# Last batch element of a DeltaNet and MLP-mixer kernel: token product by Strassen's scheme, channel products in 15 of 18 blocks over 384 tokens

## The chip, the core and the metric

The kernel runs on one core of one Trainium2 chip. The metric is the device time of one execution in microseconds. A core has a matrix engine (TensorE, "PE" in the profile; its weight loads are shown apart as "PEld"), a vector engine (VectorE, "DVE"), an activation engine (ScalarE, "ACT"), a general engine (GpSimd, "POOL") and a queue that issues DMA transfers (SyncE, "SP"). Each engine works through its own instructions in program order and waits on semaphores for the others. Matrix products land in PSUM, eight banks of 128 x 512 floats; everything else is kept in SBUF.

## The reference

Four batch elements, 8 heads, 768 tokens, head width 48. First a delta-rule recurrence gives `y`; its heads side by side are `x` (768 tokens x 384 channels). Then one mixer block works on each element:

```python
def _moe_ref(x, w_tok1, w_tok2, w_ch1, w_ch2):
    xt = x.transpose(0, 2, 1)
    h = np.maximum(xt @ w_tok1, 0.0) @ w_tok2        # over tokens: 768 -> 256 -> 768
    u = x + h.transpose(0, 2, 1)
    h2 = np.maximum(u @ w_ch1, 0.0) @ w_ch2          # over channels: 384 -> 1536 -> 384
    return (u + h2).astype(np.float32)
```

So an element has four products: the first and the second token product, and the first and the second channel product. All are in 32-bit floats.

## The kernel before

The work is written as Python generators ("jobs"): `k`, `p`, `c`, `d`, `t`, `i`, `f`, `h`, `j`, `v` load and prepare 128 tokens each, `r0` to `r47` are the steps of the recurrence (64 tokens each, twelve for an element), `w` and `s` load, round and sum weights, and `m0` to `m3` are the mixers of the four elements. A long string of job names (`order`, L1189) says which generator emits its next piece. So the order of the instructions on every engine is written out by hand, and no scheduler changes it.

`mixer(b)` (L1006) works on `xb`, the 768 x 384 block of the element as six chunks of 128 tokens:

- The first token product (L1013): 12 matrix products of 128 x 384 columns, into two PSUM banks, one for each half of the 256 hidden values. ACT takes them through a Relu into `r1` (L1021).
- The second token product (L1026): 12 products of 128 x 384; DVE adds each pair to `xb` (L1030).
- Then three pairs of chunks, 256 tokens each. PE transposes a pair (L1036), ACT copies it to `u_t` (L1040), and `forms` (L933) makes eleven sums of its 128 x 128 pieces on DVE (L954).
- The first channel product for a pair (`wide_fast`, L959, for elements 1 to 3): the weights are cut in 3 x 3 blocks and the pair in 3 x 2, and 15 block products stand for 18. Each is four matmuls of 128 columns into one bank, 60 for a pair (L985). The products run in four chains, each accumulating in its own bank; after each product the bank is read into the hidden block `r2`, by ACT as a copy (L994) or by DVE as a sum or difference (L997), and where a part is complete ACT takes the Relu (L1001). A chain's next product waits for that read.
- The second channel product for a pair: seven block products in place of eight, six matmuls of 192 columns each, 42 for a pair (L1115). The sums of hidden pieces that they need (`halves_of` and the difference of `a12`) are made on DVE (L1067), the sums of weights lie in `wc2` beside the weights (its places 4 to 6; one of the four plain blocks, place 1, is overwritten with a difference). DVE adds each result to `xb` (L1044), and SP stores the finished chunk.

`wc2` holds the second channel weights for the second channel product of every element; they were loaded as 64-bit numbers and rounded at the start by `round_weights` (L264): two ACT passes (L279, L280), a shift on DVE (L282) and an integer sum on GpSimd (L286).

In the last part of the program, `m2` (the third element's mixer) fills PE between the last steps of the recurrence, and `m3` follows. The first token product of `m3` stands right behind step `r47`, then the last 42 matmuls of `m2`, mixed with the second token product of `m3`, and then three pairs of `m3` with no other job beside them.

Of the kernel before, what the change touches and what calls it, by code (L numbers as in the profile page):

```python
# [23 lines left out]
def kernel(  # L24
# [51 lines left out]
    NHT = DCH // 128  # L76
    NM = NHT // 2
    DH = DM // 2
    NU = B * NCH
# [5 lines left out]
    work = ctx.enter_context(tc.tile_pool(name="work", bufs=2))  # L85
    mlp_pool = ctx.enter_context(tc.tile_pool(name="mlp", bufs=2))
# [24 lines left out]
    warm = const.tile([128, 129], FP32, name="warm")  # L111
# [22 lines left out]
    G = U // HB  # L134
# [13 lines left out]
    at = 0  # L148
# [47 lines left out]

    wc2 = const.tile([128, NM, 7, DH], FP32, name="wc2")
    FAST = 1
    FT = NHT // 3
    WB = FT * 128  # L200
    wcx = const.tile([128, WB // 2], FP32, name="wcx")
# [804 lines left out]
    def mixer(b):  # L1006

        xb = xbs[b]
        p_1 = [ps_mlp([128, DM], "p_1") for _ in range(NDH)]
        for c in range(NCH):  # L1010
            assert written.issuperset([NQ * b + 2 * c, NQ * b + 2 * c + 1])
            for dh in range(NDH):
                nc.tensor.matmul(  # L1013
                    p_1[dh], piece_of(w1, c, 0)[:, dh * 128 : (dh + 1) * 128], xb[:, c],
                    start=(c == 0), stop=(c == NCH - 1),
                )
            yield
        r1 = []
        for dh in range(NDH):
            r = mlp_pool.tile([128, DM], FP32, name="r1")  # L1020
            nc.scalar.activation(r, p_1[dh], ACTF.Relu)  # L1021
            r1.append(r)
        for c in range(NCH):
            p_h = ps_mlp([128, DM], "p_h")
            for j in range(NDH):
                nc.tensor.matmul(  # L1026
                    p_h, piece_of(w2, j, c * 128)[:, c * 128 : (c + 1) * 128], r1[j],
                    start=(j == 0), stop=(j == NDH - 1),
                )
            nc.vector.tensor_tensor(out=xb[:, c], in0=xb[:, c], in1=p_h, op=ALU.add)  # L1030
            yield

        def turn(u_t, c):
            p_ut = ps_mlp([128, NCB, 128], "p_ut")
            for cb in range(NCB):
                nc.tensor.transpose(  # L1036
                    p_ut[:, cb], xb[:, c, cb * 128 : (cb + 1) * 128], ident
                )
            i = c % 2 * U
            nc.scalar.copy(u_t[:, :, i : i + U], p_ut)  # L1040

        def add(c, half, p):
            e = slice(DH * half, DH * half + DH)
            nc.vector.tensor_tensor(out=xb[:, c, e], in0=xb[:, c, e], in1=p, op=ALU.add)  # L1044

        def store(c, e=slice(0, DM)):
            nc.sync.dma_start(out=out[b, c * 128 : (c + 1) * 128, e], in_=xb[:, c, e])

        def turn_pair(c):
            u_t = mlp_pool.tile([128, NCB, 2 * U], FP32, name="u_t", bufs=1)  # L1050
            for i in range(2):
                turn(u_t, c + i)
                yield
            if b < FAST:
                return u_t, None
            f = yield from forms(u_t)
            return u_t, f

        u_t, t_c = yield from turn_pair(0)
        for c in range(0, NCH, 2):  # L1060

            r2 = mlp_pool.tile([128, NM, 2, 2 * U], FP32, name="r2", bufs=1)
            a11, a12 = r2[:, :, 0, 0:U], r2[:, :, 1, 0:U]
            a21, a22 = r2[:, :, 0, U : 2 * U], r2[:, :, 1, U : 2 * U]

            def combine(out, x, y, op, ms):
                nc.vector.tensor_tensor(out=out[:, ms], in0=x[:, ms], in1=y[:, ms], op=op)  # L1067

            made = []

            def halves_of(ms):
                if not made:
                    made.extend(
                        loads.tile([128, NM, U], FP32, name=n, tag="d64", bufs=3)
                        for n in ("s1", "s2")
                    )
                s1, s2 = made
                combine(s1, a21, a22, ALU.add, ms)
                combine(s2, s1, a11, ALU.subtract, ms)
                combine(a21, a11, a21, ALU.subtract, ms)  # L1080

            if b >= FAST:
                for ms in wide_fast(t_c, r2):
                    if ms is not None:
                        halves_of(ms)
                    yield
            else:
                for m in range(NM):
                    p_c = ps_mlp([128, 2, 2 * U], "p_c")
                    for k in range(2):  # L1090
                        f = 2 * m + k
# [12 lines left out]
                    if m % (NM // 2) == NM // 2 - 1:  # L1104
                        halves_of(slice(m + 1 - NM // 2, m + 1))
                        yield

            s1, s2 = made
            turns = (*range(2, NM), 0, 1) if b >= FAST else range(NM)

            def product(p, a, j, start):
                for i, m in enumerate(turns):
                    block = (2 * m + j // 2,) if j in (0, 2, 3) else (m, "sum", j)
                    assert (id(wc2), *block) in rounded
                    nc.tensor.matmul(  # L1115
                        p, a[:, m], wc2[:, m, j],
                        start=(start and i == 0), stop=(i == NM - 1),
                        skip_group_check=True,
                    )
# [34 lines left out]
            store(c + 1, slice(0, DH) if final else slice(0, DM))  # L1154
            yield


    jobs = {}
# [12 lines left out]
    for t in range(B * NQ):  # L1171
        jobs[f"r{t}"] = recur(t)
    for b in range(B):
        jobs[f"m{b}"] = mixer(b)
    pieces = [
        piece
        for dst, src in ((w1, moe_w_tok1), (w2, moe_w_tok2), (wc1, moe_w_ch1))
# [97 lines left out]
    m2*4 r47 m2*3 r47 m2*8 r47*2 m3*5 m2 m3 m2*10 m3 m2*3 m3*6 m2 m3*3 m2 m3*158  # L1275
    """
    for word in order.split():
        name, _, n = word.partition("*")
# [34 lines left out]
```

## Time and profile before

| | before |
|---|---|
| time, median of 3 runs | 638.75 us (637.23 to 639.49) |
| the profiled execution's own time | 636.35 us |
| its span, first to last instruction | 634.6 us |
| busy share of the span: PE, DVE, ACT, POOL | 96%, 70%, 41%, 17% |
| span from the end of step r47 to the end of the program | 516.4 to 634.6 us |
| GpSimd busy after 480 us | 0.0 us |

The profile is of one execution. A 32-bit matmul stands in it as two records, so 60 matmuls are "x120" and the mean of a record is half a matmul. The view of the chain of waits follows the work that ended last back to the start; the timeline lists instructions of an engine in order of time, with the start, the length, and in brackets the idle time before it and what ended that.

### The profile page before, as it was taken

What the parts mean: (1) busy time and instruction counts of PE and PEld (TensorE: products, weight loads), DVE (VectorE), ACT (ScalarE), POOL (GpSimd) and SP (SyncE); (2) the same over time, 40 slices, a digit from 0 to 9 for tenths busy, and PEclk for the clock granted to TensorE, in tenths of its full rate; (3) what the DMA queues carried; (4) which work ended last, traced back from release to release, by engine and by line L of the source; (5) the groups of instructions that cost most, each with busy time, mean ns of one, the idle gap of its engine ahead of it and who ended that gap; (6) DMA issues with size and microseconds to landing.
All of it is one profiled execution on the core that took longest, in us unless ns stands there. A gap on an engine that the chain in (4) does not pass through costs nothing.

```text
span 634.6 us, 21586 instructions
## 1 busy us (share of the span) xinstructions
PE 609.1 (96%) x9168; PEld 526.0 (83%) x9168; DVE 443.3 (70%) x1132; ACT 258.9 (41%) x631; POOL 108.7 (17%) x147
## 2 busy tenths in 40 slices
PE   9679898999999999999999999999999999999997
PEld 5448676677898988858899999769999978899997
DVE  3986776977889758897969997588627252473643
ACT  6848886436422332215615332244333230223240
POOL 1447364242400211011111110001000000000000
PEclk9988999999999999999999999999999999999999
DMA  9966777555442444435444222311020000000000
GB/s 173 205 132 136 163 155 186 128 125 141 102 120 52 97 108 77 107 76 119 90 91 93 43 84 41 75 17 27 14 50 7 28 1 13 13 1 25 2 26 26
DMA packets 135776, 50.27 MB, mean 79 GB/s; under 512 B 114656, under 2 KB 130144, under 8 KB 135680
## 3 DMA queue, kind: packets, MB, share of 16 engines
q1 hardware_dynamic: 135680, 48.89, 34.7%
q8 instruction: 72, 1.18, 0.8%
q14 instruction: 24, 0.20, 0.1%
HBM read 39.42 MB, written 9.44 MB: 77 GB/s over the span
## 4 chain that ended last, share of the span: by engine, by line
PE 74%; DVE 10%; ACT 5%; DMA 5%; issue 3%; SPq 2%; POOL 0%; DVEq 0%; ACTq 0%; POOLq 0%
PE p_o L1115 26%; PE p_r L985 18%; PE p_c L1093 6%; PE p L1013 4%; PE p_h L1026 3%; PE p_s L855 2%; PE p_y L837 2%; PE p_k L817 2%; DVE x L680 2%; DVE sub L676 2%; PE p_g L442 2%; PE p_warm L227 1%; DMA kst<-in_k_dram 1%; DMA gm<-w_dram 1%; PE p_z L775 1%
## 5 line engine op out<-in xcount | busy, mean ns | idle before, releaser
L1115 PE MATMUL p_o<-wc,r 128*128 128x192 f32 x720 | 127.0, 329 | 0.6 <-ACT u_t L1040 0.6
L1115 PEld LDWEIGHTS p_o<-wc,r 128*128 128x128 f32 x720 | 116.7, 190 | 3.0 <-ACT u_t L1040 1.1
L997 DVE TENSOR_TENSOR r<-r,p_r 128x512 f32<-128x512 f32 x90 | 59.6, 682 | 35.1 <-PE p_r L985 32.9
L1044 DVE TENSOR_TENSOR xb<-xb,p_o 128x192 f32<-128x192 f32 x84 | 29.2, 350 | 59.7 <-PE p_o L1115 59.5
L680 DVE TENSOR_TENSOR x<-x,sub 128x84 f32<-128x84 f32 (+24 forms) x178 | 60.3, 339 | 6.1
L994 ACT COPY r<-p_r 128x512 f32<-128x512 f32 x54 | 31.5, 585 | 80.6 <-PE p_r L985 77.2
L676 DVE TENSOR_TENSOR sub<-x 128x84 f32<-128x84 f32 (+24 forms) x178 | 57.5, 323 | 9.5 <-DMA x<-n_dram 5.6
L1115 PE MATMUL p_o<-wc,s 128*128 128x192 f32 x288 | 51.2, 330 | 0.3 <-DVE xb L1044 0.3
L1093 PE MATMUL p_c<-u_t,wc 128*128 128x256 f32 x216 | 50.5, 385 | 0.0
L416 POOL TENSOR_TENSOR v_st<-v_st,nrm 128x384 f32<-128x384 f32 x24 | 21.0, 874 | 167.7 <-DMA v_st<-in_v_dram 96.1
L1115 PEld LDWEIGHTS p_o<-wc,s 128*128 128x128 f32 x288 | 46.7, 190 | 1.3 <-DVE xb L1044 0.6
L869 ACT ACTIVATE xb<-p_y 64x192 f32<-64x192 f32 x96 | 31.1, 324 | 39.9 <-PE p_y L856 28.9
L1001 ACT ACTIVATE r<-r 128x512 f32<-128x512 f32 x54 | 33.9, 630 | 28.3 <-DVE r L997 28.0
L1093 PEld LDWEIGHTS p_c<-u_t,wc 128*128 128x128 f32 x216 | 39.8, 190 | 5.4
L499 POOL TENSOR_TENSOR mb<-mask_c,cs 128x512 f32<-128x512 f32 x20 | 21.1, 1053 | 117.7 <-DVE cs L478 94.9
L442 PE MATMUL p_g<-kq 48*64 48x128 f32 (+1 forms) x704 | 37.5, 279 | 3.1 <-ACT kq L511 2.4
L985 PE MATMUL p_r<-u_t,wc 128*128 128x128 f32 x288 | 38.5, 277 | 0.0
L985 PE MATMUL p_r<-t_d,wc 128*128 128x128 f32 x288 | 37.5, 281 | 0.3 <-DVE r L997 0.3
L985 PEld LDWEIGHTS p_r<-u_t,wc 128*128 128x128 f32 x288 | 35.3, 192 | 0.3
L985 PEld LDWEIGHTS p_r<-t_d,wc 128*128 128x128 f32 x288 | 34.0, 191 | 1.3 <-DVE r L997 0.4
L1026 PE MATMUL p_h<-r,w 128*128 128x384 f32 x96 | 33.7, 494 | 0.0
L1013 PE MATMUL p<-xb,w 128*128 128x384 f32 x96 | 33.6, 495 | 0.0
(176 smaller groups left out, 1205.0 us busy)
## 6 DMA issues: line engine op xcount, KB each, us to landing
d<-in_moe_w_ch_dram SPq DMA_DIRECT2D x24, 384.0 KB, 4.0
v_st<-in_v_dram SPq DMA_DIRECT2D x96, 48.0 KB, 2.8
out_dram<-xb SPq DMA_DIRECT2D x23, 192.0 KB, 1.9
kst<-in_k_dram SPq DMA_DIRECT2D x64, 48.0 KB, 3.0
n_dram<-gm SPq DMA_DIRECT2D x72, 32.0 KB, 1.9
pads<-in_k_dram SPq DMA_DIRECT2D x24, 96.0 KB, 3.4
pads<-in_q_dram SPq DMA_DIRECT2D x24, 96.0 KB, 2.7
gm<-w_dram SPq DMA_DIRECT2D x72, 32.0 KB, 2.1
```

The lines of the kernel that those rows point to most:

```text
L442: nc.tensor.matmul(p_g[PAR[i ^ cc], p], kqt[f, p, cc, 0], kqt[f, p, cc])
L676: nc.vector.tensor_tensor(out=tmp, in0=col.to_broadcast(dims), in1=row.to_broadcast(dims), op=ALU.mult,)
L680: nc.vector.tensor_tensor(out=new, in0=new, in1=tmp, op=ALU.add)
L869: nc.scalar.mul(y[:, :, D * i : D * i + D], p_y[PAR[1 - i]], 1.0 if c else -1.0)
L985: nc.tensor.matmul(p[:, i], pieces[i // width][:, at : at + 128], f[f"u{n}"], start=first and i == 0, stop=True, skip_group_check=True,)
L994: nc.scalar.copy(o, p)
L997: nc.vector.tensor_tensor(out=o, in0=o, in1=p, op=ALU.add if sign > 0 else ALU.subtract)
L1001: nc.scalar.activation(o, o, ACTF.Relu)
L1013: nc.tensor.matmul(p_1[dh], piece_of(w1, c, 0)[:, dh * 128 : (dh + 1) * 128], xb[:, c], start=(c == 0), stop=(c == NCH - 1),)
L1026: nc.tensor.matmul(p_h, piece_of(w2, j, c * 128)[:, c * 128 : (c + 1) * 128], r1[j], start=(j == 0), stop=(j == NDH - 1),)
L1093: nc.tensor.matmul(p_c[:, k], piece_of(wc1, cb, f * 128)[:, f * 128 : (f + 1) * 128], u_t[:, cb], start=(cb == 0), stop=(cb == NCB - 1),)
L1115: nc.tensor.matmul(p, a[:, m], wc2[:, m, j], start=(start and i == 0), stop=(i == NM - 1), skip_group_check=True,)
```

## The change

For the last element alone, `mixer` is replaced by `last_mixer`. The other elements are as before.

- **First token product**: `x` in 2 x 2 blocks (chunks 0 to 2 and 3 to 5, columns 0 to 191 and 192 to 383), seven block products of three matmuls of 128 x 192 each, 21 matmuls for 12 of 384 columns. Weight sums are made on GpSimd (job `A`), sums of `x` on GpSimd for all chunks but the last, on DVE for that.
- **Channel products**: two groups of 384 tokens in place of three pairs of 256. The first product is the same 15 of 18 blocks at 192 columns; since four times 192 columns don't fit one bank, each chain has two banks. The second product takes 15 of 18 blocks as well, of 128-token, 512-value and 192-column blocks, in place of seven of eight.
- **Sums for them**: sums of the transposed `u` for the first group on DVE, for the second group on GpSimd; sums of the second channel weights (job `Q`, 12 of 128 x 768) on GpSimd; sums of the hidden blocks (15 of 128 x 512 for a group) on GpSimd, but four of the second group's on DVE.
- **Weights loaded again**: place 1 of `wc2` holds a difference, so jobs `G0` to `G2` load half the columns of half the weights again (six DMAs), round them on ACT and DVE and write them with GpSimd. The write may come only when `m2` has read place 1 for the last time.

```diff
@@ mixer @@
-            final = (b, c) == (B - 1, NCH - 2)
-            if final:
-                store(c + 1, slice(DH, DM))
+            if b == last - 1:
+                o_done.append(True)
...
+    def restore(m):
...
+        for k in range(2):
+            nc.sync.dma_start(out=d64[:, k], in_=rows[:, m + k, 0, DH:DM])
+        yield
...
+        nc.scalar.activation(a, a, ACTF.Prelu, scale=2.0**-112, alpha=2.0**32)
+        nc.scalar.activation(lo, lo, ACTF.Copy, scale=2.0**-29)
+        yield
+        nc.vector.tensor_scalar(
+            out=f, in0=hi, scalar1=3, scalar2=None, op0=ALU.logical_shift_left,
+        )
+        yield
+        assert len(o_done) == 3
+        nc.gpsimd.tensor_tensor(
+            out=wc2[:, m : m + 2, 1].bitcast(U32), in0=f, in1=lo, op=ALU.add
+        )
...
+    def out_sums():
...
+            ("u12", b[1, 0], b[2, 0], add), ("u10", b[0, 0], b[2, 0], add),
+            ("u6", b[0, 1], b[0, 0], sub), ("u3", b[0, 1], b[1, 1], add),
+            ("u2", "u3", b[0, 0], sub), ("u4", b[1, 0], "u2", sub),
+            ("u5", b[0, 0], b[2, 1], add), ("u13", "u12", b[2, 1], sub),
+            ("u8", "u13", b[1, 1], sub), ("u7", none, b[0, 1], sub),
+            ("u7", "u7", b[2, 1], sub), ("u15", b[2, 0], b[2, 1], sub),
...
+            eng = nc.vector if out in SUMS_V else nc.gpsimd
...
+    SUMS_V = ('none',)
+    FORMS_V = (('none',), ('w15', 'w9'))
+
+    ORDER = (
+        (1, 1, ((0, 0, 1, 0),)), (4, 12, ((0, 0, -1, 0),)), (2, 5, ((2, 0, 1, 0),)),
+        (1, 2, ((0, 1, 1, 0),)), (4, 13, ((0, 1, -1, 0),)), (2, 6, ((2, 1, 1, 0),)),
+        (1, 3, ((1, 1, 1, 0),)), (4, 14, ((2, 1, 1, 0),)), (1, 4, ((1, 0, 1, 0),)),
+        (2, 7, ((1, 1, 1, 1),)), (3, 10, ((1, 0, 1, 1), (2, 0, -1, 0))),
+        (2, 8, ((2, 1, -1, 1),)), (4, 15, ((2, 0, 1, 1),)), (3, 11, ((0, 0, 1, 1),)),
+        (2, 9, ((0, 1, 1, 1),)),
+    )
+
+    def last_mixer():
...
+        def wide(q, f):
...
+                if first:
+                    ps = {1: ps_mlp, 4: ps_seq, 2: ps_prep, 3: ps_mlp}[chain]
+                    banks[chain] = [ps([128, 2, DH], f"q_r{chain}") for _ in range(2)]
...
+                    nc.tensor.matmul(
+                        banks[chain][i // 2][:, i % 2],
+                        pieces[i // width][:, at : at + 128], f[f"u{n}"],
+                        start=first and i % 2 == 0, stop=True, skip_group_check=True,
+                    )
+                yield
+                for j, e, sign, fin in reads:
+                    for h, p in enumerate(banks[chain]):
+                        o = hid[q][j][:, 2 * h : 2 * h + 2, DH * e : DH * e + DH]
+                        if (j, e) not in begun:
+                            assert sign == 1
+                            nc.scalar.copy(o, p)
+                        else:
+                            tt(v, o, o, p, add if sign > 0 else sub)
...
+        def a_forms(q):
...
+                tt(v if out in by_v[q] else g, f[out], x, y, op)
...
+        def outs(q, f):
...
+                    nc.tensor.matmul(
+                        p, f[f"w{n}"][:, i], o_w[f"u{n}"][:, i // 2, i % 2],
+                        start=first and i == 0, stop=True, skip_group_check=True,
+                    )
+                yield
+                for j, e, sign, fin in reads:
+                    c = HT * q + j
+                    o = xb[:, c, DH * e : DH * e + DH]
+                    tt(v, o, o, p, add if sign > 0 else sub)
...
@@ order @@
-    m2*16 r45*4 m2*6 j23 m2 v23 m2 r46*4 m2*2 r46*2 m2*2 r46*3 m2*6 r47 r46 r47*4
+    m2*10 A*4 m2*6 r45*4 m2*6 m3*2 j23 m2 v23 m2 m3 r46*4 m2*2 r46*2 m2*2 m3 r46*3
+    m2*6 r47 r46 G0 G1 G2 r47*4 m2*4 m3*2 r47 m2*3 G0*2 r47 m2*4 G1*2 m2*4 G2
...
```

Where the change moves instructions, three places matter. **ACT around step r47.** `L870` (before: `L869`) writes the step's result to `xb`, `L1002` (before: `L1001`) is the Relu of `m2`'s last hidden block, `L848` (before: `L847`) copies the step's `w_t`. Before:

```order
L1001 ACTIVATE r_7307<-r_7307 128x4x128 x2
L847 COPY w_t<-p_w 128x192
L1001 ACTIVATE r_7307<-r_7307 128x4x128 x4
L869 ACTIVATE xb<-p_y 64x4x48 x2
L1021 ACTIVATE r_7543<-p_7486 128x384
```

In the change, at the same place:

```order
L1002 ACTIVATE r_7311<-r_7311 128x4x128 x2
L1232 ACTIVATE pads<-pads 128x384
L1233 ACTIVATE pads<-pads 128x384
L848 COPY w_t<-p_w 128x192
L1002 ACTIVATE r_7311<-r_7311 128x4x128 x2
L1232 ACTIVATE pads<-pads 128x384
L1233 ACTIVATE pads<-pads 128x384
L1002 ACTIVATE r_7311<-r_7311 128x4x128 x2
L1232 ACTIVATE kq_99<-kq_99 128x384
L1233 ACTIVATE kq_99<-kq_99 128x384
L870 ACTIVATE xb<-p_y 64x4x48 x2
```

The six passes that round the reloaded weights (L1232, L1233) now stand between the Relus, one pair of them ahead of `w_t` and all ahead of the write of `xb`. On DVE the shifts of `G0` and `G1` (L1235) stand between the reads of the same hidden block, `G0`'s ahead of the last four reads and `G1`'s ahead of the last two.

**PE behind step r47**, whose last products are `p_y`. Before, the 12 matmuls of the token product (`L1013`, two banks in turn) stand between them and `m2`'s last products; the first two of the 12:

```order
L985 MATMUL p_r<-u_t,lent 128x128 x4
L985 MATMUL p_r<-u_t,wc_126 128x128 x4
L856 MATMUL p_y<-w_t,gm 64x48 x8
L1013 MATMUL p_7486<-xb,w_124 128x384
L1013 MATMUL p_7487<-xb,w_124 128x384
```

In the change seven of the 21 matmuls of the token product (`q_a`, `q_b`) stand ahead of these rows, and the rest among `m2`'s last products (`p_o`):

```order
L857 MATMUL p_y<-w_t,gm 64x48 x8
L1118 MATMUL p_o<-wc_127,r_7311 128x192 x6
L1118 MATMUL p_o_7528<-wc_127,r_7311 128x192 x6
L1317 MATMUL q_b<-xb,w_124 128x192
L1317 MATMUL q_a<-gm,kq_99 128x192
L1118 MATMUL p_o<-wc_127,s_7520 128x192 x6
L1317 MATMUL q_b<-gm,kq_99 128x192 x3
L1118 MATMUL p_o_7528<-wc_127,s_7519 128x192 x6
L1317 MATMUL q_a<-gm,w_124 128x192 x3
L1317 MATMUL q_b<-xb,kq_99 128x192 x3
L1118 MATMUL p_o<-wc_127,r_7311 128x192 x6
L1317 MATMUL q_a<-gm,w_124 128x192 x3
```

`m2`'s last products have moved forward, from behind the whole token product to directly behind the step.

**GpSimd at the end.** Before, its last rows are those of `v_st` for step r47; nothing follows. In the change, from that row on (`L1240` the write of reloaded weights, `L1274` job `Q`, the last `L1299` the sums of the second group's `u`; 26 sums of hidden blocks follow):

```order
L417 TENSOR_TENSOR v_st<-v_st,nrm_103 128x384
L1299 TENSOR_TENSOR gm<-xb 128x576
L1299 TENSOR_TENSOR gm<-xb,gm 128x384
L1299 TENSOR_TENSOR gm<-xb 128x384
L1299 TENSOR_TENSOR gm<-xb,gm 128x384
L1240 TENSOR_TENSOR wc_127<-pads 128x2x192
L1240 TENSOR_TENSOR wc_127<-gm,pads 128x2x192
L1274 TENSOR_TENSOR gm<-wc_127 128x768 x4
L1274 TENSOR_TENSOR gm<-gm,wc_127 128x768
L1274 TENSOR_TENSOR gm<-wc_127,gm 128x768
L1240 TENSOR_TENSOR wc_127<-gm,kq_99 128x2x192
L1274 TENSOR_TENSOR gm<-wc_127 128x768
```

The third `L1240` reads what DVE's third shift (L1235) makes, and that shift stands on DVE behind the eleven sums of the first group's `u`, so GpSimd stops there after six sums of job `Q` until those are made.

More of the change, by code (lines that the diff above doesn't have):

```diff
@@ L198 @@
     FAST = 1
+    last = B - 1
     FT = NHT // 3
@@ L1153, in mixer, with cut_of @@
             add(c + 1, 0, p_o)
-            store(c + 1, slice(0, DH) if final else slice(0, DM))
+            store(c + 1)
             yield
+    a_sums = {}
+    R3 = NCH // 2
+    HT = 3
+    gm_flat = gmb.rearrange("s b n -> s (b n)")
+    kq_flat = [kq.rearrange("f i p e n -> f (i p e n)") for kq in kq_of]
+    pads_flat = pads.rearrange("s i e n -> s (i e n)")
+    def cut_of(flat, at, shape):
+        n = 1
+        for x in shape:
+            n *= x
+        flat = flat[:, at : at + n]
+        if len(shape) == 1:
+            return flat
+        if len(shape) == 2:
+            return flat.rearrange("p (a n) -> p a n", a=shape[0])
+        return flat.rearrange("p (a b n) -> p a b n", a=shape[0], b=shape[1])
@@ new lines, in winograd_a, with token_sums @@
+    def winograd_a(out, a11, a12, a21, a22):
+        s1, s2, d = out
+        for o, x, y, op in (
+            (s1, a21, a22, ALU.add), (s2, s1, a11, ALU.subtract),
+            (d, a12, s2, ALU.subtract), (a21, a11, a21, ALU.subtract),
+        ):
+            nc.gpsimd.tensor_tensor(out=o, in0=x, in1=y, op=op)
+            yield
+        return
+    def token_sums():
+        u = last * NCH + 1
+        assert token_done and 2 * u + 1 in keyed and u in asked
+        assert turned.issuperset(((True, NU - 1), (False, NU - 1)))
+        x, a = a_sums[1]["sums"], a_sums[1]["raw"]
+        for i, _ in enumerate(winograd_a(x, *a)):
+            if i == 3:
+                a_sums["made"] = True
+            yield
@@ new lines @@
+    o_w = {}
+    def out_sums():
+        assert walked.issuperset(range(B * NQ))
+        b = {
+            (k, e): wc2[:, 2 * k : 2 * k + 2, e:4:2] for k in range(3) for e in range(2)
+        }
+        names = ("u5", "u12", "u3", "u2", "u6", "u13", "u4", "u8", "u10")
+        n = 4 * DH
+        f = {z: cut_of(gm_flat, i * n, (2, 2, DH)) for i, z in enumerate(names)}
+        f.update(
+            u7=b[0, 1], u15=b[2, 0], u1=b[0, 0], u9=b[1, 1], u11=b[1, 0], u14=b[2, 1]
+        )
+        add, sub = ALU.add, ALU.subtract
+        none = warm[:, 0:1][:, None, None, :].to_broadcast([128, 2, 2, DH])
+        for out, x, y, op in (
+            ("u12", b[1, 0], b[2, 0], add), ("u10", b[0, 0], b[2, 0], add),
[4 more added lines that the diff above has]
+            ("u7", "u7", b[2, 1], sub), ("u15", b[2, 0], b[2, 1], sub),
+        ):
+            assert len(whole) >= {"u12": 0, "u10": 0, "u6": 1}.get(out, 2)
+            assert len(whole) == 3 or y is not b[2, 1]
+            x, y = (f[z] if isinstance(z, str) else z for z in (x, y))
+            eng = nc.vector if out in SUMS_V else nc.gpsimd
+            eng.tensor_tensor(out=f[out], in0=x, in1=y, op=op)
+            o_w.update({z: f[z] for z in ("u1", "u9", "u11", "u14")})
+            if x is not none:
+                o_w[out] = f[out]
+            yield
@@ L1173 @@
     for b in range(B):
-        jobs[f"m{b}"] = mixer(b)
+        jobs[f"m{b}"] = mixer(b) if b < last else last_mixer()
+    jobs["A"] = token_sums()
+    for i in range(3):
+        jobs[f"G{i}"] = restore(2 * i)
+    jobs["Q"] = out_sums()
     pieces = [
```

271 lines of the change are left out of this document (270 added, 1 removed).

## Prediction

> **What bounds the kernel now.** I read the page first, then the chain of waits over the part that the change touches, then the timeline at its gaps.
>
> ```profile
> span 634.6 us, 21586 instructions
> PE 609.1 (96%) x9168; PEld 526.0 (83%) x9168; DVE 443.3 (70%) x1132; ACT 258.9 (41%) x631; POOL 108.7 (17%) x147
> ```
>
> PE is busy nearly always, so time is won by fewer or cheaper matmuls, and every wait put in front of PE costs its full length. The chain of waits (start, length, what) from the end of step r47 on:
>
> ```profile
> 516.45 7.94 PE p L1013 x24
> 524.39 8.78 PE p_o L1115 x54
> 537.38 6.45 PE p_h L1026 x20
> 543.83 0.33 PE p_ut L1036 x3
> 546.44 13.67 PE p_r L985 x120
> 563.01 12.07 PE p_o L1115 x72
> 575.08 13.67 PE p_r L985 x120
> 591.65 12.07 PE p_o L1115 x72
> 603.73 13.68 PE p_r L985 x120
> 617.43 0.70 DVE r L997
> 621.57 10.03 PE p_o L1115 x60
> 631.62 0.35 DVE xb L1044
> ```
>
> From this a record of 192 columns costs 8.78 / 54 = 0.1626 us, of 128 columns 13.67 / 120 = 0.1139, of 384 columns 6.45 / 20 = 0.3225; a transpose costs 0.11. The chain runs over DVE from 617.43 to 621.57, but PE isn't idle there, as the timeline says:
>
> ```profile
> 563.01 2.22 PE L1115 MATMUL p_o<-wc,r 128*128 128x192 f32 x12 [0.29 <-ACT u_t L1040]
> 617.23 4.07 PE L1115 MATMUL p_o<-wc,r 128*128 128x192 f32 x24
> 621.57 4.17 PE L1115 MATMUL p_o<-wc,s 128*128 128x192 f32 x24 [0.27 <-DVE xb L1044]
> ```
>
> PE did 24 records meanwhile and lost 0.27 us. It loses 0.29 us for `u_t` in each of the first two pairs. That is all the visible waiting after r47, so little is to be won from gaps.
>
> **What goes.**
>
> - First token product: 7.94 us now; 21 matmuls are 42 records, 42 x 0.1626 = 6.83. Gain 1.11.
> - First channel product: 360 records of 128 columns take 13.67 + 13.67 + 13.68 = 41.02 us; 120 matmuls of 192 columns are 240 records, 39.02. Gain 2.00. The columns are as many (360 x 128 = 240 x 192); the gain is that short records cost more for a column.
> - Second channel product: 126 matmuls become 120, 12 records less. Gain 1.95.
> - Waits seen: 2 x 0.29 + 0.27 = 0.85. Behind each group's products PE now finds the other group's.
> - Slower stretches: 72 records took 12.07 against 72 x 0.1626 = 11.71, twice, and the last 60 took 10.03 against 9.76; together 0.99. They stand at changes of bank. New code has many such changes, so I take half, 0.5; bounds 0 and 1.0.
>
> Together 6.4 us. The second token product stays, and so do the 18 transposes.
>
> The Trainium skill ("TensorE: Matmul & The Clock Gate", Back-to-back issue gap) gives N / 2.4 + 2.5 ns as the gap of a single warm matmul; if a record counts as two, my estimate is 0.112 us at 128 columns and 0.165 at 192, so that the second item would gain 0.6 us instead of 2.0. The trace's 0.1139 and 0.1626 differ from that in both directions, and the trace decides.
>
> **What comes: ACT and DVE at step r47.** Seven matmuls (14 records, 2.28 us) stand ahead of the step's last products, so everything there comes 2.28 us later; that is paid inside the 6.83 above. The timeline there, before:
>
> ```profile
> 511.41 0.63 ACT L1001 ACTIVATE r<-r 128x512 f32<-128x512 f32 x1 [1.10 <-DVE r L997]
> 513.11 0.63 ACT L1001 ACTIVATE r<-r 128x512 f32<-128x512 f32 x1 [1.07 <-DVE r L997]
> 513.65 0.30 ACT L847 COPY w_t<-p_w 128x192 f32<-128x192 f32 x1
> 517.27 0.66 ACT L869 ACTIVATE xb<-p_y 64x192 f32<-64x192 f32 x2
> 512.39 3.30 DVE L997 TENSOR_TENSOR r<-r,p_r 128x512 f32<-128x512 f32 x5 [1.01 <-PE p_r L985]
> 514.80 1.06 PE L985 MATMUL p_r<-u_t,wc 128*128 128x128 f32 x8
> 516.38 2.85 PE L1013 MATMUL p<-xb,w 128*128 128x384 f32 x8
> ```
>
> What a rounding costs, from the same instructions at the start of the program (min/median/max ns):
>
> ```profile
> L279 ACT ACTIVATE d<-d x34: 427/558/572, 4.4 to 166.2; 128x384 f32<-128x384 f32 x28, 128x256 f32<-128x256 f32 x6
> L280 ACT ACTIVATE d<-d x34: 417/548/579, 4.8 to 166.7; 128x384 uint32<-128x384 uint32 x28, 128x256 uint32<-128x256 uint32 x6
> L282 DVE TENSOR_SCALAR w_f<-d x34: 282/352/704, 4.9 to 170.0; 128x384 uint32<-128x384 uint32 x28, 128x256 uint32<-128x256 uint32 x6
> ```
>
> So a pair of ACT passes takes 1.11 us and a DVE shift 0.35. Working the queues through:
>
> 1. The second Relu ends at 513.74 + 2.28 = 516.02. `G0`'s passes follow, to 517.13; DVE's shift, to 517.48; only then DVE's read of the block product whose bank the last product needs (0.66), to 518.14. That product stood at 514.80 + 2.28 = 517.08. **PE waits 1.06 us**, and the step's products end at 516.38 + 2.28 + 1.06 = 519.72.
> 2. DVE's next read ends at 518.80, two Relus at 519.45, `G1`'s passes at 520.56, the shift at 520.91, the last two reads at 521.57 and 522.23, the Relus for them at 522.20 and 522.88. PE has begun `m2`'s last products at 519.72, does four matmuls (1.30 us) and needs the fifth Relu. **It waits 1.2 us**, where before the token product's 7.94 us covered this.
> 3. `G2`'s passes end at 523.99, the write of `xb` at 524.65. The first matmul on the last chunk needs it at about 524.8: no wait. The next needs a sum on DVE, which stands behind six sums of hidden blocks; these rows time them, from 618.04 to 621.16:
>
> ```profile
> 618.04 0.68 DVE L1067 TENSOR_TENSOR s<-r 128x512 f32<-128x512 f32 x1
> 620.83 0.42 DVE L1067 TENSOR_TENSOR r<-r 128x256 f32<-128x256 f32 x1
> 621.16 0.81 DVE L1044 TENSOR_TENSOR xb<-xb,p_o 128x192 f32<-128x192 f32 x2
> ```
>
> 3.12 us from 522.23 is 525.35; an add and the sum (about 0.3 each) bring it to 525.98, and PE has been free since 525.15. **It waits 0.8 us.**
>
> Together 3.1 us. The bounds are 0 (if the passes slip into ACT's idle 1.10 and 1.07 us) and 6.3 (if a rounding's passes and shift, 1.46 us, and one more Relu, 0.63, held PE at each of the three places). I take the worked 3.1, as its rows come from this very stretch. The DMAs for the reload are issued after `m2`'s second pair is stored, about 499 us; that 1.2 MB is due at 516, on queues that are nearly empty.
>
> After that a product has its sums in time. In the first channel product DVE reads two banks of 128 x 384, each about 0.55 by the `p_h` adds below, 1.1 us for a product that takes PE 8 x 0.1626 = 1.30.
>
> ```profile
> L1030 DVE TENSOR_TENSOR xb<-xb,p_h 128x384 f32<-128x384 f32 x6 | 3.3, 554 | 5.9 <-PE p_h L1026 5.9
> ```
>
> **GpSimd.** These groups price it (mean ns before the bar's end):
>
> ```profile
> L286 POOL TENSOR_TENSOR wc<-w_f,d 128x384 uint32<-128x384 uint32 x24 | 25.3, 1061 | 40.9 <-DVE w_f L282 18.1 <-ACT d L280 6.7 <-issue 5.7
> L499 POOL TENSOR_TENSOR mb<-mask_c,cs 128x512 f32<-128x512 f32 x20 | 21.1, 1053 | 117.7 <-DVE cs L478 94.9 <-DVE gm L445 21.9 <-DMA d<-in_moe_w_tok_dram 0.8
> L416 POOL TENSOR_TENSOR v_st<-v_st,nrm 128x384 f32<-128x384 f32 x24 | 21.0, 874 | 167.7 <-DMA v_st<-in_v_dram 96.1 <-DMA gm<-w_dram 20.6 <-DVE t_d L954 18.7
> L286 POOL TENSOR_TENSOR w<-w_f,d 128x256 uint32<-128x256 uint32 x6 | 4.4, 735 | 19.4 <-ACT d L280 9.6 <-ACT wc L491 9.2 <-ACT gm L731 0.6
> ```
>
> 128 columns more cost 1053 - 874 = 179 ns in float and 1061 - 735 = 326 in the strided integers. That puts 768 columns at 1.4 to 2.0 us and 512 at 1.05 to 1.4. No row shows two dense float inputs; both ends stay. Some 5 us after the first group's first product starts, GpSimd goes on with a write (1.1), job `Q`'s other six sums (8.4 to 12.0) and the first of eleven sums of 192 columns (under 0.9, the 256-column row plus its slope); that one is due 21 us after the same start and comes at 15 to 19, the other ten are wanted 1.3 us apart. The first group's 15 hidden sums take 16 to 21, beside 19.5 us of PE in the second group's product; the first is wanted at its end, and the last 18 us later. So GpSimd costs nothing in the forecast.
>
> **The sum.** Gain 6.4, loss 3.1, net 3.3 us: the profiled execution's 636.35 us (1.75 around its span) would be 633.0. The median of the runs is 2.4 us above that execution, so the median becomes 638.75 - 3.3 = **635.4 us**; by the bounds of the forecast's own terms 632 to 638.7.
>
> **Rivals.**
>
> *The sums on VectorE meet GpSimd* (the slower side). The rows show what a meeting costs:
>
> ```profile
> 121.04 0.40 DVE L680 TENSOR_TENSOR x<-x,sub 128x234 f32<-128x234 f32 x1
> 121.84 2.16 POOL L286 TENSOR_TENSOR wc<-w_f,d 128x384 uint32<-128x384 uint32 x2 [5.69 <-issue]
> 122.05 1.08 DVE L680 TENSOR_TENSOR x<-x,sub 128x228 f32<-128x228 f32 x1
> 123.06 0.68 DVE L445 TENSOR_TENSOR gm<-p_g,mb 128x512 f32<-128x512 f32 x1
> ```
>
> With both inputs in SBUF a DVE sum of 0.40 took 1.08 beside GpSimd, ending with GpSimd's instruction; with one input in PSUM (`p_g`) it took its usual 0.68. The Trainium skill ("SBUF — State Buffer", SBUF: two separate sides) has it as an exclusive lock on a shared port pair, held for a whole instruction, by a GpSimd operation or a VectorE one with two SBUF inputs; the trace agrees. The eleven sums of the first group's `u` have two SBUF inputs. GpSimd may begin the reload's write when `m2` has read place 1 for the last time; from there to DVE's first such sum PE has 30 records of 192, 24 of 384 and nine transposes, 4.9 + 7.7 + 1.0, and an add: 14.2 us. GpSimd has two writes (2.1) and six sums (8.4 to 12.0): 10.5 to 14.1, just clear. They meet from 2.0 us a sum; the GpSimd time left then goes into DVE's queue, of which PE covers about 1 us. From 2.7 us (18.3 in all, 4.1 late) the gain is gone, and at 3.2 (21.3, 7.1 late) 6.1 us are lost: 638.75 - 3.3 + 6.1 = 641.5. Against it: 2.7 is well over the rows' upper end.
>
> *The queues at r47 cost 6.3, not 3.1*: 638.6, no change to speak of. For it: every Relu, read and pass there is in one chain through two queues. Against it: the passes' rows are steady (548 to 572).
>
> *The queues hide them* and all slow stretches go: 638.75 - 6.9 = 631.9. For it: ACT's idle 1.10 and 1.07 us; against it: the passes stand behind Relus in program order.
>
> *The change doesn't get its sums off the path*: the second group's hidden sums come late. They start with the first group's last; 23 sums are wanted within 37 us, so it decides at 1.6 us each, against 1.05 to 1.4. At 1.7 the price is about 2 us, and DVE's four sums there wait too: 638.5.
>
> **Chances.** Forecast 0.62, meeting 0.07, dearer queues 0.14, hidden queues 0.12, late sums 0.05. The range takes the forecast's bounds and reaches to the dearer queues and nearly to the hidden ones: 632.0 to 638.8. A measurement of this kernel tells about 0.3% (1.9 us) from no change: faster takes 0.58 of the forecast's chance and the hidden queues', 0.70; the same takes 0.04 of the forecast's, 0.12 of the dearer queues' and half of the late sums', 0.18; slower the rest, 0.12.
>
> **What would show it.** Right: a span near 631; records of 192 columns at 0.163 in all of `q_r` and `q_o`; three short idle times of PE between r47's end and the second token product, 3 us in all; none over 0.3 us behind it; DVE's eleven sums at about 0.35 each. Wrong: DVE's eleven sums at over 1 us beside GpSimd, PE waiting for POOL at the second group's first products, GpSimd sums of 512 columns over 1.6 us, or the first channel product's records above 0.17.

## The result and the profile after

In the first timing the changed kernel takes 630.93 us (median of four runs, 629.99 to 633.96) against 638.87: a ratio of 0.9888, 95% interval 0.9848 to 0.9928. In a second timing on one chip, beside the experiments, it takes 632.98 (eight runs, 627.8 to 635.15) against 637.6 (25 runs): 0.9926, interval 0.9898 to 0.9954. So the change makes the kernel faster, by 4.6 to 7.9 us by the two medians, where 3.3 was forecast. The profiled execution took 631.77 us:

```profile
span 630.0 us, 21470 instructions
PE 605.4 (96%) x9054; PEld 525.7 (83%) x9054; DVE 437.9 (70%) x1120; ACT 261.9 (42%) x642; POOL 179.8 (29%) x207
```

GpSimd has 71 us more work than before; PE is as full as it was. To compare two kernels I use marks in the chain of waits. Before (first line), and after (the others):

```profile
495.33 3.12 PE p_o L1115 x18
```

```profile
495.81 3.12 PE p_o L1118 x18
...
547.85 1.30 PE q_r L1450 x8
...
552.74 35.10 PE q_r L1450 x216
587.84 39.01 PE q_o L1505 x240
626.88 0.35 DVE xb L1299
```

The first mark is the start of `m2`'s last 18 records ahead of the steps r46 and r47; how far it moves from run to run is shown with the first experiments. The **changed stretch** runs from it to the start of the last add on DVE: before 631.62 - 495.33 = 136.29 us, after 626.88 - 495.81 = 131.07. That is 5.22 us less, in two parts. From the mark to the first wide product it is 52.04 after and 546.44 - 495.33 = 51.11 before: **0.93 us longer**, of which three transposes that stood behind this point before make 0.33. From there to the end it is 79.03 against 85.18: **6.15 us shorter**, and in it 216 and 240 records run at 0.1625 us each with no wait.

What PE waits for around step r47, in the timeline (brackets: idle time and what ended it):

```profile
518.00 1.16 PE L986 MATMUL p_r<-u_t,wc 128*128 128x128 f32 x8 [0.27 <-DVE r L998]
519.68 4.54 PE L1118 MATMUL p_o<-wc,r 128*128 128x192 f32 x24
524.05 0.49 PE L1317 MATMUL q_b<-xb,w 128*128 128x192 f32 x2
524.88 0.59 PE L1317 MATMUL q_a<-gm,kq 128*128 128x192 f32 x2 [0.34 <-DVE gm L1299]
```

The three places of the forecast are there: in front of the last block product 0.27; inside the 24 records that start at 519.68, which reach to 524.05, 4.37 us for 24 x 0.1626 = 3.90, 0.47 lost; and 0.34 for `t5`. Visible are 1.1 us, where 3.1 were forecast.

GpSimd's new work, by group (busy us, mean ns before the bar's end):

```profile
L1274 POOL TENSOR_TENSOR gm<-wc 128x768 f32<-128x768 f32 x5 | 8.9, 1804 | 0.1
L1299 POOL TENSOR_TENSOR kq<-kq 128x512 f32<-128x512 f32 x6 | 7.6, 1274 | 0.2
L1299 POOL TENSOR_TENSOR wc<-wc 128x192 f32<-128x192 f32 x11 | 6.2, 599 | 0.2
```

768 columns take 1.80 us (forecast 1.4 to 2.0), 512 take 1.27 (1.05 to 1.4), 192 take 0.60 (under 0.9). No wait of PE in the changed stretch ends with GpSimd.

### The profile page after: what moved, and what is told of

The parts are those of the page before. It is cut to its first block, busy times and chain, and to the rows that moved or that the text cites. A ratio compares the mean times of both kernels' runs of the same rounds, so it can differ in the third digit from the quotient of the medians.

```text
span 630.0 us, 21470 instructions
## 1 busy us (share of the span) xinstructions
PE 605.4 (96%) x9054; PEld 525.7 (83%) x9054; DVE 437.9 (70%) x1120; ACT 261.9 (42%) x642; POOL 179.8 (29%) x207
## 4 chain that ended last, share of the span: by engine, by line
PE 81%; DVE 7%; DMA 4%; ACT 4%; SPq 2%; issue 2%; DVEq 0%; ACTq 0%
PE p_o L1118 20%; PE p_r L986 11%; PE p_c L1096 7%; PE q_o L1505 6%; PE q_r L1450 6%; PE p L1014 4%; PE p_h L1027 3%; PE p_g L443 3%; PE p_k L818 3%; PE p_s L856 3%; PE p_y L838 3%; PE p_warm L228 2%; DMA kst<-in_k_dram 2%; PE p_w L842 1%; PE p_z L776 1%
## 5 line engine op out<-in xcount | busy, mean ns | idle before, releaser
L1118 PE MATMUL p_o<-wc,r 128*128 128x192 f32 x540 | 96.4, 330 | 0.1
L1118 PEld LDWEIGHTS p_o<-wc,r 128*128 128x128 f32 x540 | 87.5, 190 | 2.2 <-ACT r L1002 0.4
L998 DVE TENSOR_TENSOR r<-r,p_r 128x512 f32<-128x512 f32 x60 | 39.5, 682 | 16.3 <-PE p_r L986 16.0
L870 ACT ACTIVATE xb<-p_y 64x192 f32<-64x192 f32 x96 | 31.1, 324 | 39.2 <-PE p_y L857 28.2
L287 POOL TENSOR_TENSOR wc<-w_f,d 128x384 uint32<-128x384 uint32 x24 | 25.3, 1059 | 42.3 <-DVE w_f L283 14.6
L848 ACT COPY w_t<-p_w 128x192 f32<-128x192 f32 x48 | 15.2, 316 | 46.2 <-PE p_w L842 45.8
L443 PEld LDWEIGHTS p_g<-kq 48*64 48x64 f32 (+1 forms) x704 | 27.1, 135 | 8.4 <-ACT kq L512 3.8
L818 PEld LDWEIGHTS p_k<-s_t,kq 48*64 48x64 f32 x656 | 24.0, 136 | 10.6 <-DVE s_t L865 5.1
L838 PEld LDWEIGHTS p_y<-s_t,kq 48*64 48x64 f32 x656 | 24.3, 136 | 10.0 <-issue 7.0
L818 PE MATMUL p_k<-s_t,kq 48*64 48x48 f32 x656 | 29.5, 225 | 2.7 <-DVE s_t L865 2.6
L446 DVE TENSOR_TENSOR gm<-p_g,mb 128x512 f32<-128x512 f32 x44 | 29.3, 684 | 3.7 <-PE p_g L443 3.1
```

The source lines that it names most:

```text
L443: nc.tensor.matmul(p_g[PAR[i ^ cc], p], kqt[f, p, cc, 0], kqt[f, p, cc])
L818: nc.tensor.matmul(p_k[r, p], kqt[f, p, cc, 0], s0[f, p])
L838: nc.tensor.matmul(p_y[o, p], kqt[f, p, cc, 1], s0[f, p], start=(p == 0), stop=False,)
L870: nc.scalar.mul(y[:, :, D * i : D * i + D], p_y[PAR[1 - i]], 1.0 if c else -1.0)
L998: nc.vector.tensor_tensor(out=o, in0=o, in1=p, op=ALU.add if sign > 0 else ALU.subtract)
L1118: nc.tensor.matmul(p, a[:, m], wc2[:, m, j], start=(start and i == 0), stop=(i == NM - 1), skip_group_check=True,)
```

## The experiments

All kernels but `meet` compute the same thing. The intervals are those of the ratio to the kernel before on the same chip.

**Each kernel once more.** The changed kernel:

> The changed kernel as it stands, in five rounds. Theory A (what the two profiles show in the changed stretch is all there is): from step r45's copy of `w_t`, 486 us, to the end the two profiles differ by 5.1 us, and nothing ahead of that differs by kernel, so the ratio is about 0.992 (-5.1 us), and the stretch takes 143.2 us again. Rival B (the first medians' -7.9 us is the change's own worth, the rest of it somewhere ahead of 486 us): the ratio is about 0.988 again, and the marks ahead of 486 us stand earlier than before's.

The kernel before against itself:

> The kernel before against itself: its ratio should hold 1 within 0.002, and its profile gives a second copy of the early marks. Theory A expects the stretch from step r45's copy of `w_t` to the end at 148.2 us again and the mark itself to differ from 486.35 us by some us of chance; rival B expects that mark at or behind 486 us and after the mark of the changed kernel of the same chip by 2 to 3 us.

The changed kernel has the ratio 0.9926 (0.9898 to 0.9954), the kernel before 1.0004 (0.9982 to 1.0027). In the second profiles the changed stretch is 627.73 - 496.67 = 131.06 us after and 630.83 - 494.53 = 136.30 before, within 0.01 us of the first ones; from step r45's copy of `w_t` to the end it is 143.1 us (487.69 to 630.8) and 148.2 (485.56 to 633.8), as expected. Theory A holds. The mark itself stands at 495.33 and 494.53 in the two profiles of before and at 495.81 and 496.67 in those of the changed kernel, no earlier with the change, so rival B falls. The mark moves with what happens at the start of the program. Two kernels further down, whose code up to there differs in the place of six DMAs and their passes near 480 us alone, have marks 5.07 us apart (493.57 and 498.64), and 4.4 us of that are there at a copy of `w_t` that starts at 144.78 in the one and at 149.16 in the other. The windows view from 0 to 130 us shows that their granted clocks differ (the column ahead of the last two); `token_old`:

```profile
0.00:130.00 130.00, 111.81 (x2322) 82.02 (x2323) 100.25 (x271) 91.77 (x245) 55.54 (x76) 0.96 0.75 161
```

`token_old_early`:

```profile
0.00:130.00 130.00, 112.58 (x2301) 83.76 (x2302) 96.18 (x259) 91.25 (x243) 55.68 (x76) 0.91 0.71 155
```

A twentieth of clock over 130 us is at most 6.5 us. The clock is not all of it: in the two profiles of before the same view has 0.96 and 0.93, and the mark of the second, with the lower clock, is the earlier one. What else moves the mark stays open. That is the noise in which a kernel's time stands; the changed stretch repeats to 0.01 us.

**The reload's passes away from step r47.**

```diff
-    m2*10 A*4 m2*6 r45*4 m2*6 m3*2 j23 ...
-    m2*6 r47 r46 G0 G1 G2 r47*4 m2*4 m3*2 r47 m2*3 G0*2 r47 m2*4 G1*2 m2*4 G2
+    m2*10 A*4 G0 G1 G2 m2*6 r45 G0*2 G1*2 G2 r45*3 m2*6 m3*2 j23 ...
+    m2*6 r47 r46 r47*4 m2*4 m3*2 r47 m2*3 r47 m2*4 m2*4
```

> Changed kernel with the reload's DMAs issued ahead of step r45 and its six ACT passes and the first two DVE shifts moved there, where ACT had 8.7 us of idle time. Theory: PE's waits at r47 (0.27 us in front of the last block product, 0.45 us inside the products behind it, 0.34 us for the sum t5) come from those passes and shifts in the queues; the first two go and the third shrinks, 0.7 to 1.4 us faster than the changed kernel. Rival: Relus and DVE's reads alone make the waits, or the moved loads and passes cost as much at r45: within 0.3 us of the changed kernel.

0.9887 (0.986 to 0.9914); median 629.85 us beside the changed kernel's 632.98 on the same chip. ACT in the new place, and PE behind r47:

```profile
485.98 0.33 ACT L848 COPY w_t<-p_w 128x192 f32<-128x192 f32 x1
486.19 0.58 ACT L1232 ACTIVATE pads<-pads 128x384 f32<-128x384 f32 x1
...
488.43 0.56 ACT L1233 ACTIVATE kq<-kq 128x384 uint32<-128x384 uint32 x1
495.05 0.66 ACT L870 ACTIVATE xb<-p_y 64x192 f32<-64x192 f32 x2 [6.05 <-PE p_y L857]
```

```profile
518.29 4.17 PE L1118 MATMUL p_o<-wc,r 128*128 128x192 f32 x24
522.29 0.49 PE L1317 MATMUL q_b<-xb,w 128*128 128x192 f32 x2
522.62 0.49 PE L1317 MATMUL q_a<-gm,kq 128*128 128x192 f32 x2
```

Six passes end 6 us ahead of the next work of ACT, and the three waits of PE are gone, the third too, which was expected only to shrink (24 records from 518.29 to 522.29 are 0.1 over 3.90). By the chain, the first wide product starts 50.53 us behind the mark, and the stretch is 129.55:

```profile
494.96 3.12 PE p_o L1118 x18
...
545.49 1.30 PE q_r L1450 x8
...
624.51 0.35 DVE xb L1299
```

So the passes cost the changed kernel **1.52 us** (131.07 - 129.55), a little over the 0.7 to 1.4 expected. By PE's timelines, each counted from its mark, the three places cost 0.54, 0.37 and 0.61 us: the first wait is shown as 0.27 us of idle time and costs twice that, the last as 0.34. In their new place the passes and their DMAs stand ahead of the mark, where the stretch doesn't count them. But from an ACT copy ahead of those DMAs (469.80, and 470.65 in the changed kernel) to the mark in PE's timeline (494.89 and 495.74) it is 25.09 us in both, so they cost nothing there. The medians differ by 3.1, and the intervals of the two ratios overlap; the stretch, which repeats, says 1.5. By it this version beats both kernels.

**The old token product**, with the reload late and early:

```diff
-            nc.gpsimd.tensor_tensor(out=o, in0=x, in1=y, op=op)   # job A
...
+        p_1 = [ps_mlp([128, DM], "p_1") for _ in range(NDH)]
+        for c in range(NCH):
+            for dh in range(NDH):
+                nc.tensor.matmul(p_1[dh], w1[:, c, dh * 128 : (dh + 1) * 128], xb[:, c], ...)
```

> Changed kernel with the first token product made as before (24 matmuls of 384 columns behind the reload's passes), the channel products and the reload as changed. Theory: it loses the token product's 1.1 us and gets back only the wait for t5 (0.34 us), so it is 0.5 to 1.0 us slower than the changed kernel. Rival: the new token product's waits eat its gain, as the first wide product's start suggests (0.9 us later than before's): it is as fast, or up to 0.9 us faster.

> The old token product together with the early reload, the fourth corner of a square. From the start of the last 18 output products of the third pair (495.33 us in the profile of before) to the first wide product it is 51.1 us before, 52.0 changed, 50.5 with the early reload, 53.3 with the old token product. Theory (the two edits do not touch each other; old product 7.94, no waits, one more set of three transposes of 0.11 ahead of that mark than before): 51.4 us, 0.9 slower than the new product with the early reload. Rival (the old product hides the queues or meets other waits): 50.5 or less, or 52 and more.

Ratios 0.9958 (0.9937 to 0.9978) and 0.9918 (0.9874 to 0.9963). The chain of `token_old`:

```profile
493.57 3.12 PE p_o L1118 x18
...
546.85 1.30 PE q_r L1414 x8
```

and of `token_old_early`:

```profile
498.64 3.12 PE p_o L1118 x18
...
550.36 1.30 PE q_r L1414 x8
```

From the mark to the first wide product:

| | passes at r47 | passes at r45 |
|---|---|---|
| old token product | 53.28 us | 51.72 us |
| new token product | 52.04 us (the change) | 50.53 us |

The new product is worth 1.24 and 1.19 us, against 1.11 by its records; the passes at r47 cost 1.56 and 1.51, whichever product stands there. The two edits do not touch each other. For the early corner 51.4 was expected and 51.7 came. For the late one I expected a loss of 0.5 to 1.0 us, which was too little: I let the old product win back the wait for `t5`, and it has a wait of its own in place of it, 0.39 us of idle time in front of an output product, for an add of DVE to `xb`.

**GpSimd beside DVE's eleven sums.** The first attempt moved the third reload's write and six weight sums ahead of them:

```diff
-    ... m2*2 G0 G1 Q*6 m3 m2*2 m3*4 m2*2
-    m3*10 G2*2 Q*6 m3*120
+    ... m2*2 G0 G1 Q*6 G2*2 Q*6 m3 m2*2 m3*4 m2*2
+    m3*10 m3*120
```

> Changed kernel with the third reload's shift and write and the last six weight sums of GpSimd put ahead of the eleven DVE sums of the first group in program order, so that GpSimd works on 768 columns while DVE makes them. Theory (a DVE sum with both inputs in SBUF waits for GpSimd's instruction, as at 122.05 us): these sums take over 1 us each beside GpSimd, PE waits for several of them, and the stretch from the first wide product to the end (82.15 us in the changed kernel) grows by 3 to 10 us. Rival (two dense float sums do not meet): sums at 0.35 us and 82.2 us again.

This kernel answers another question: the sums moved stand ahead of `m2`'s last product in program order and overwrite weight blocks that it reads, so that this product is made with other weights, and PE waits for them:

```profile
557.86 1.65 PE L1118 MATMUL p_o<-wc,r 128*128 128x192 f32 x4 [20.58 <-POOL wc L1274]
```

1.0333 (1.0303 to 1.0363). When DVE came to its eleven sums GpSimd was idle; nothing follows on the meeting. The second attempt lengthens GpSimd's work where it stands:

```diff
             eng.tensor_tensor(out=f[out], in0=x, in1=y, op=op)
+            if out in ("u3", "u2", "u4"):
+                eng.tensor_tensor(out=f[out], in0=x, in1=y, op=op)
```

> Changed kernel with three of GpSimd's first six weight sums (`u3`, `u2`, `u4`) issued twice: 5.4 us more from 547.2 us on, so that GpSimd works on 768 columns until 552.7 while DVE makes its eleven sums from 548.4 (in the changed kernel it is idle there). By the forecast's rival of a meeting the GpSimd time left at 548.4 goes into DVE's queue, less 1 us of cover: the stretch from the first wide product to PE's end grows by 3.3 us. By the run with the doubled hidden sums, where a DVE sum beside GpSimd took 1.49 instead of 0.69 us and GpSimd's 1.7 instead of 1.27, the two take turns: three or four sums are made by 553, one is wanted every 1.6 us, and 0.5 to 2 us are lost. If they do not meet: nothing, and sums of 0.35 us.

0.9969 (0.9928 to 1.0009). The timelines of DVE, GpSimd and PE at that place:

```profile
548.87 4.76 DVE L1301 TENSOR_TENSOR a_x<-gm 128x192 f32<-128x192 f32 x3
553.66 0.36 DVE L1301 TENSOR_TENSOR a_x<-a_x,gm 128x192 f32<-128x192 f32 x1
```

```profile
547.81 1.81 POOL L1276 TENSOR_TENSOR gm<-gm,wc 128x768 f32<-128x768 f32 x1
549.71 1.81 POOL L1274 TENSOR_TENSOR gm<-wc,gm 128x768 f32<-128x768 f32 x1
551.60 1.81 POOL L1276 TENSOR_TENSOR gm<-wc,gm 128x768 f32<-128x768 f32 x1
```

```profile
554.07 1.57 PE L1452 MATMUL q_r<-a_x,lent 128*128 128x192 f32 x8 [0.39 <-DVE a_x L1301]
556.81 2.87 PE L1452 MATMUL q_r<-a_x,wc 128*128 128x192 f32 x16 [1.17 <-DVE kq L1301]
```

Three sums of 0.35 us take 4.76 beside GpSimd, one for each of its instructions, and keep their 0.36 when it has ended. By the chain's mark (496.31) and last add (629.91) the stretch is 133.60 us, 2.53 longer: between the two forecasts of a meeting (0.5 to 2, and 3.3). In the changed kernel the last of GpSimd's six sums and DVE's first stand so:

```profile
545.40 1.81 POOL L1274 TENSOR_TENSOR gm<-wc,gm 128x768 f32<-128x768 f32 x1
```

```profile
548.36 0.89 DVE L1299 TENSOR_TENSOR a_x<-gm 128x192 f32<-128x192 f32 x3
```

GpSimd ends at 547.21 (545.40 + 1.81), so they miss each other by 1.2 us.

**Hidden sums: dearer on GpSimd, and all on DVE.**

```diff
                 tt(v if out in by_v[q] else g, f[out], x, y, op)
+                if out in ("w12", "w11", "w3", "w2", "w5"):
+                    tt(g, f[out], x, y, op)
```

> Changed kernel with the first five hidden sums of each group issued twice on GpSimd, 10 instructions of 1.27 us more. Theory (GpSimd works without pause from 570.0 us and the second group's `w1`, 23 sums later, is wanted at 607.35): 33 x 1.27 = 41.9, so `w1` comes at 611.9 and the end is 4.6 us later, all of it as one wait of PE in front of the second group's first output product. Rival (the sums have more slack, or PE waits for other sums first): under 1 us, or waits already in the first group's product.

1.0043 (0.9995 to 1.0091). The timelines of PE, DVE and GpSimd where the second group's output product starts, and the clock there by the windows view:

```profile
612.20 2.93 PE L1507 MATMUL q_o<-wc,r 128*128 128x192 f32 x8 [6.50 <-POOL r L1299]
```

```profile
609.53 1.49 DVE L1299 TENSOR_TENSOR pads<-pads 128x512 f32<-128x512 f32 x1
```

```profile
610.43 1.71 POOL L1299 TENSOR_TENSOR r<-r,pads 128x512 f32<-128x512 f32 x1
```

```profile
612.20:616.60 4.40, 4.40 (x14) 4.40 (x15) 2.52 (x4) 0.00 (x0) 4.32 (x3) 0.50 0.12 45
```

One wait at the place named, with nothing ahead of it; it is 6.50 us long, not 4.6. By the timeline GpSimd's instructions start 1.30 us apart (31 from 568.38 to 608.70), where I took 1.27, and the last two meet DVE's hidden sums: 1.71 us in place of 1.27 on GpSimd, 1.49 in place of 0.68 on DVE. The stretch grew by more than the wait: 634.45 - 494.16 = 140.29, 9.22 us more. Behind the wait PE has half its clock for some 4.4 us (0.50 in the last row), which is where most of the other 2.7 goes.

```diff
-    FORMS_V = (('none',), ('w15', 'w9'))
+    FORMS_V = (h, h)   # h: all the names
```

> Changed kernel with all fifteen hidden sums of both groups on DVE instead of GpSimd. By listed durations DVE has 15 x 0.685 + 20 x 0.552 = 21.3 us to do while PE has 19.5 us of products, so the first group's output product would wait about 1.8 us. By the spacing at which back-to-back DVE instructions start (0.60 for 512 columns, 0.47 for 384) it has 18.4 us, and nothing is lost: within 0.3 us of the changed kernel. The first is the way in which the waits at r47 were forecast, the second the way in which this study explains that they came out smaller.

0.9936 (0.9892 to 0.9979). By mark (497.76) and last add (628.87) the stretch is 131.11 us, 0.04 more than in the changed kernel. DVE's timeline late in the second group's first channel product, beside which it now makes the first group's hidden sums:

```profile
586.34 0.68 DVE L1299 TENSOR_TENSOR kq<-kq 128x512 f32<-128x512 f32 x1
586.94 1.01 DVE L1299 TENSOR_TENSOR pads<-pads,q_r 128x384 f32<-128x384 f32 x2
587.87 0.68 DVE L1299 TENSOR_TENSOR kq<-kq,kq 128x512 f32<-128x512 f32 x1
```

A sum listed at 0.68 is followed by the next instruction after 0.60, two reads listed at 0.55 each by the next after 0.93. Having the sums on GpSimd gains no time here. But the run doesn't decide between the two ways of counting, as was meant. PE starts the first group's output product at 589.63, when DVE has made twelve of the fifteen sums (the last starts at 592.46), and it needn't wait: its first block product reads `w1`, the eighth of them. Eight sums and twenty reads fit into 19.5 us by listed durations too (8 x 0.685 + 20 x 0.552 = 16.5).

## Why the prediction was right and wrong

- **What goes**: right, and only its last term too small. The gains were 1.11 + 2.00 + 1.95 + 0.85 + 0.5 = 6.4 us. With the passes out of the way the change is worth 136.29 - 129.55 = 6.74; so 0.34 more goes than forecast.
- **Slower stretches**: mis-sized. "New code has many such changes, so I take half": 0.5. But 216 and 240 records in a row take 0.1625 each, across all their changes of bank. From the first wide product on, 6.15 us went, 0.33 of it transposes that now stand ahead: 5.82, against 2.00 + 1.95 + 0.85 + 0.99 = 5.79. So the whole 0.99 went. "They stand at changes of bank" was the wrong reason: in before's timeline the last 36 of the 72 records from 563.01 take 5.85 us, 0.1625 each, and most of the excess is what the wait for `u_t` costs over its idle time. Ahead of it six transposes and the wait take 1.11 us (561.90 to 563.01) where 0.66 + 0.29 are listed, and the 12 records behind it 2.06 in place of 1.95. The waits at r47 cost more than their idle time in the same way.
- **What comes at r47**: the step that failed. The mechanism was right: passes and shifts in the queues make PE wait at the three places named, and without them PE doesn't wait. The size was 3.1 us (1.06, 1.2 and 0.8) and is 1.52 (0.54, 0.37 and 0.61). Two things made it too large. The larger is a wait that isn't there: twice the chain puts DVE's shift behind both of ACT's passes ("`G0`'s passes follow, to 517.13; DVE's shift, to 517.48"). By the code of the change the shift reads the high words, which the first pass writes, and the second pass works on the low ones. ACT's and DVE's timelines at r47 in the changed kernel:

```profile
515.87 0.63 ACT L1002 ACTIVATE r<-r 128x512 f32<-128x512 f32 x1 [2.38 <-DVE r L998]
516.41 0.54 ACT L1232 ACTIVATE pads<-pads 128x384 f32<-128x384 f32 x1
516.85 0.55 ACT L1233 ACTIVATE pads<-pads 128x384 uint32<-128x384 uint32 x1
517.30 0.30 ACT L848 COPY w_t<-p_w 128x192 f32<-128x192 f32 x1
```

```profile
516.99 0.36 DVE L1235 TENSOR_SCALAR pads<-pads 128x384 uint32<-128x384 uint32 x1 [0.55 <-ACT pads L1232]
519.68 0.36 DVE L1235 TENSOR_SCALAR gm<-pads 128x384 uint32<-128x384 uint32 x1 [1.14 <-ACT pads L1232]
```

  The first shift starts at 516.99, right behind the first pass (516.41 + 0.54; the bracket names its line, L1232) and before the second ends (516.85 + 0.55). My estimate, the forecast's own chain with its listed durations and the shift behind the first pass alone: waits of 0.5, 0.6 and 0.85, 2.0 us in all. So 1.1 us of the error is this wait. The other 0.5 fits the second thing, though no run tests it by itself: I added listed durations, and a listed duration is not the time until the next start. A pair of passes is listed at 1.09 and delays the next instruction by 0.89; a Relu of 0.63 by 0.54; a DVE sum of 0.68 by 0.60. The Trainium skill says it in two places: "Perfetto Trace Analysis" (Optimizing Scalar/DVE Operations) has half of the fixed latency that a profile shows for an instruction overlapping with the next one, and "Vector Engine (DVE) Microarchitecture Reference" (5.2, Measured stream behaviour on trn2) gives 1.0417 ns a column and about 75 ns for back-to-back DVE instructions; my estimate by that page is 0.61 us for 512 columns and 0.475 for 384, and the rows' 0.60 and 0.47 agree.
- **The sum**: 6.74 - 1.52 = 5.22 us in place of 6.4 - 3.1 = 3.3. From the median of before that makes 633.5, inside the range, though 1.9 us below the forecast. The first median, 630.93, lies lower than any of my cases, and what separates it from 633.5 the changed stretch doesn't show; the second timing (4.6 us) lies on its other side. The profiles have differences of that size ahead of the mark, at the start of the program (marks up to 5.07 us apart); that the first medians differ for the same reason is likely and not shown, as only one run of each was profiled.
- **"GpSimd costs nothing"**: right, by 1.2 us at the eleven sums. The forecast had 10.5 to 14.1 us of work against 14.2 ("just clear"); it was 12.8 (534.38 to 547.21) against 14.0.
- **Rivals**: the meeting is real (`meet2`) but does not occur; late hidden sums are real beyond 1.6 us each (`slow_g` waits where that rule puts it), against 1.27. The dearer queues did not come. "The queues hide them", 631.9, was nearer to the first median than the forecast, for another reason: the queues cost half, they do not vanish.

## What to carry over

Ahead of adding up a chain over two queues, look up which instruction each one waits for: a shift put behind two passes, where it reads the result of the first, made 1.1 of 3.1 us, where 1.5 came. Add up a queue by the distance between starts of back-to-back instructions, not by listed durations. Compare kernels of which one stage changed by that stage between marks in the chain of waits: it repeated to 0.01 us, where the difference of the medians moved by 3. Work off the critical path is put where its engine idles *and* no one waits behind it; the same six passes cost 1.5 us at r47 and nothing 30 us earlier.

## What the runs showed of the hardware

PE's wait of 6.5 us in `slow_g` was followed by a granted clock of 0.50 for 4.4 us, and the wait of 20.6 us in `meet` by the same:

```profile
557.90:562.50 4.60, 4.60 (x10) 3.08 (x11) 0.68 (x2) 0.00 (x0) 1.67 (x1) 0.50 0.12 43
```

The longest wait in the other kernels' stretches, 1.17 us in `meet2`, was not. The Trainium skill ("TensorE: Matmul & The Clock Gate", What's actually happening) has the clock halved after an idle window of about 3.4 us; the runs agree on both sides of it. So a long wait is dearer than it looks: 9.2 us for 6.5. And a DVE sum of two SBUF inputs beside GpSimd got one turn for each GpSimd instruction, 1.6 us each in place of 0.35, while GpSimd's 1.81 stayed as it was (`meet2`); with 512 columns on both, in `slow_g`, both took longer, 1.49 in place of 0.68 on DVE and 1.71 in place of 1.27 on GpSimd.
